# A two-layer FNet and GEGLU kernel on one core: layer 0's last two row blocks multiply by wh as a pair, and accumulators are begun by ScalarE's copies

## The chip, the core and the metric

The program runs on one core of a Trainium2 chip. The core has a matrix engine (TensorE, PE in the profile; its weight loads stand apart as PEld), a vector engine (VectorE, DVE), an activation engine (ScalarE, ACT), a general engine (GpSimd, POOL) and a queue engine that mostly issues DMAs (SyncE, SP). Each engine takes its own instructions in order and waits on semaphores for the others. Tiles lie in SBUF, 128 partitions wide; TensorE writes its products to PSUM, which the program uses as eight banks of 128 x 512 float32, and a group of matmuls may add up in one bank.

The metric is the device time of one execution in microseconds, the median over runs. Less is better.

## The reference

Four layers on x of 2048 rows and 512 columns, float32, each with a layer norm ahead and a residual: Fourier mixing, GEGLU, mixing, GEGLU.

```python
def _layernorm(x, axis=-1, eps=1e-5): ...
def _A_ref(x, dft_seq_re, dft_seq_im, dft_hid_re, dft_hid_im):
    a = einsum("bsd,ed->bse", x, dft_hid_re)
    b = einsum("bsd,ed->bse", x, dft_hid_im)
    return einsum("ts,bse->bte", dft_seq_re, a) - einsum("ts,bse->bte", dft_seq_im, b)
def _B_ref(x, w_gate, w_up, w_down):            # 512 -> 1792 -> 512
    return (_gelu(x @ w_gate) * (x @ w_up)) @ w_down
x = x + _A_ref(_layernorm(x), ...)
x = x + _B_ref(_layernorm(x), ...)
x = x + _A_ref(_layernorm(x), ...)
x = x + _B_ref(_layernorm(x), ...)
```

## The kernel before

**Products.** Every float32 product is made of three matmuls: each operand is split into a high part (a copy by ScalarE to the matmul's type, line 126) and the rest (a subtraction on VectorE, line 128), and `mm3` multiplies high by high, high by low and low by high (lines 166 to 168). A matmul has 128 x 128 weights and mostly 512 moving columns.

**Seven instead of eight.** Most large products are done by Winograd's form of a 2 x 2 block product: seven block products, named A11, A12, S1, S2, S3, S4 and A22, with sums and differences of blocks (`plus`, `minus`, lines 157 and 154, on VectorE) before and after. S1, S2, S3 and S4 are sums of the left operand's blocks, T1 to T4 those of the right one's.

**Mixing (`mix`, layers 0 and 2).** The rows of the result are done in four blocks b = 0 to 3 of 512. First the sequence product, by seven products over NK = 8 chunks: A11 and A12 for all four blocks ahead (in layer 0 in one sweep over the rows, `fore`, 384 matmuls), whose sums for blocks 1 to 3 are put away in DRAM (`put_away`, tensors m and m_sum) and fetched back later; then, block by block, `s2` (S2, S1, S3; 144 matmuls) and `s4` (S4, A22; 96). Where TensorE's product has to be added to an earlier sum, VectorE adds it (`based`, line 157). Then the hidden product by wh: `hid_groups` does a block's four row tiles by eight 128-row chunks of wh, 4 x 8 x 3 = 96 matmuls, into four banks, and `x_add` adds the rows of x and writes them out. Where a block and the next are named in `PAIRED`, the two blocks' products by wh are instead one more 2 x 2 block product (`pair_products`): seven products over four chunks of 128 and two halves, 7 x 4 x 2 x 3 = 168 matmuls. Its right operand's parts lie ready in DRAM (tensor wp), made earlier by `weight_steps`, and its results are transposed by VectorE in 32 x 32 pieces and added to turned rows of x (`turned_rows`). Before, layer 2 has two pairs and layer 0 none.

**Sums of the sequence weights.** A block's S1 to S4 are the same in layers 0 and 2. For the block named in `STORED` layer 0 writes them to DRAM (tensors S1 to S4, 32 writes of 256 KB by GpSimd's queue) and layer 2 loads them; for the others layer 2 forms them anew.

**GEGLU (`geglu`, layers 1 and 3, two halves w = 0 and 1 of 1024 rows).** Gate/up goes over 14 weight blocks n, each seven products of six matmuls: A11 into bank `chain`, S2 on top of it, S1 into `side`, then S3, S4, A12 (`second`) and A22. A11's and A12's product of the next block are done between (`first(n + 1)`, `second(n + 1)`). The split weights of a block are made once, in layer 1's first half (`weight_steps`, four `divide` steps), and written to DRAM (tensor wb) for the three later halves, which load them two blocks ahead (`piece_load`). Down goes the same way, its weights in tensor wc.

**Order.** The program is written as one sequence with side work hung in: after each product `step()` takes one entry from `queue`, and each `PACE`-th time one from `slow`. A planner then lays down each engine's order from modelled durations when the program is built; no engine reorders afterwards (TensorE's weight loads apart). Loads of weights run `AHEAD` and `RAW` items ahead of their use.

## Time and profile before

| | |
|---|---|
| time, median of 3 runs (lowest, highest) | 1589.49 us (1589.01, 1591.12) |
| span of the profiled execution, first to last instruction | 1587.3 us |
| its own time beside the span | not given apart; the median of the runs is 2.2 us above the span |
| TensorE, VectorE, ScalarE, GpSimd busy | 1579.0, 1250.1, 875.4, 253.6 us |
| matmuls in the records | 7000 (22 of them warm the engine up) |
| DMA | 427 MB, 269 GB/s over the span |

By TensorE's count the stages lie in the span about so: layer 0's opening sweep to 95 us, the rest of its mixing to 400 us, layer 1's halves to 600 and 800 us, layer 2's mixing to 1181 us, layer 3's halves to 1381 us and the end. A row of a stretch reads: busy time of each engine with its instructions, then granted clock, DMA share and GB/s. A row of waits names the engine and line that waited, who ended it, total us, times and the longest.

### The profile page before, as it was taken

How to read it: one execution, taken by the hardware profiler on the slowest of the kernel's cores; microseconds unless marked ns; L12 is line 12 of the kernel's file. 1: busy time of each engine (PE TensorE's matmuls, PEld its weight loads, DVE VectorE, ACT ScalarE, POOL GpSimd, SP SyncE). 2: the span in 40 equal slices, each digit the busy share in tenths (PEclk: the TensorE clock that was granted, in tenths of full speed). 3: DMA queues.
4: the chain of work that ended last, by engine and by line, in shares of the span. 5: the costliest groups of instructions: out<-in, count | busy, mean ns of one | idle time of the engine just before them, and what ended most of it. 6: DMA issues, size and time to landing. Idle time of an engine off the chain costs nothing.

```text
span 1587.3 us, 23208 instructions
## 1 busy us (share of the span) xinstructions
PE 1579.0 (99%) x7000; PEld 1307.6 (82%) x7000; DVE 1250.1 (79%) x2174; ACT 875.4 (55%) x1714; POOL 253.6 (16%) x445
## 2 busy tenths in 40 slices
PE   9999999999999999999999999999999999999998
PEld 7888888888888888888888888888888888888887
DVE  8999999889699795566969997869985458754475
ACT  7864574645676652746768444566546435433361
POOL 2200324311465201230031000021002000000001
PEclk9999999999999999999999999999999999999999
DMA  9946989987999999996976785789998967896463
GB/s 360 332 150 232 361 270 362 335 286 259 328 344 345 297 329 301 288 331 221 310 238 217 270 229 172 233 283 309 279 327 239 297 198 238 293 289 197 135 197 81
DMA packets 257660, 427.04 MB, mean 269 GB/s; under 512 B 33344, under 2 KB 89408, under 8 KB 256512
## 3 DMA queue, kind: packets, MB, share of 16 engines
q1 hardware_dynamic: 228560, 333.28, 66.2%
q0 software_dynamic: 26544, 91.51, 15.7%
q8 instruction: 55, 0.90, 0.2%
q10 hardware_dynamic: 2432, 0.79, 0.2%
q14 instruction: 69, 0.57, 0.1%
HBM read 335.02 MB, written 90.44 MB: 268 GB/s over the span
## 4 chain that ended last, share of the span: by engine, by line
PE 96%; DVE 2%; DMA 2%; issue 0%; ACT 0%; SPq 0%; DVEq 0%; ACTq 0%
PE p L166 32%; PE p L167 32%; PE p L168 32%; DMA s<-ws 1%; DVE s L128 1%; DVE s L154 0%; DMA s<-x 0%; DVE s L157 0%; DVE xwide L154 0%; ACT s L126 0%; DVE wide L154 0%; SPq L302 0%; SPq L194 0%; ACT s L572 0%; DVE wide L157 0%
## 5 line engine op out<-in xcount | busy, mean ns | idle before, releaser
L167 PE MATMUL p<-s,s 128*128 128x512 f32 x2326 | 899.8, 388 | 0.0
L168 PE MATMUL p<-s,s 128*128 128x512 f32 x2326 | 887.6, 388 | 0.0
L166 PE MATMUL p<-s,s 128*128 128x512 f32 x2326 | 872.5, 388 | 2.0 <-ACT s L126 1.5
L126 ACT ACTIVATE s<-s 128x512 fp32r<-128x512 f32 (+1 forms) x868 | 487.4, 608 | 319.8 <-DVE s L154 108.7
L128 DVE TENSOR_TENSOR s<-s,s 128x512 fp32r<-128x512 f32 (+1 forms) x868 | 546.0, 669 | 58.2 <-ACT s L126 54.0
L166 PEld LDWEIGHTS p<-s,s 128*128 128x128 f32 x2326 | 436.7, 188 | 94.2 <-ACT s L126 3.4
L167 PEld LDWEIGHTS p<-s,s 128*128 128x128 f32 x2326 | 436.8, 188 | 89.7 <-DVE s L128 0.5
L168 PEld LDWEIGHTS p<-s,s 128*128 128x128 f32 x2326 | 436.6, 188 | 89.4
L157 DVE TENSOR_TENSOR s<-s,p 128x512 f32<-128x512 f32 (+1 forms) x293 | 196.2, 682 | 189.6 <-PE p L168 109.5
L154 DVE TENSOR_TENSOR s<-s,s 128x512 f32<-128x512 f32 (+1 forms) x414 | 249.8, 623 | 2.8 <-DMA s<-ws 0.9
L161 ACT ACTIVATE s<-p 128x512 f32<-128x512 f32 x252 | 146.9, 592 | 147.0 <-PE p L168 142.0
L1079 ACT ACTIVATE s<-s 128x512 f32<-128x512 f32 x112 | 70.3, 629 | 121.5 <-DVE s L157 121.0
L247 POOL DMA_DIRECT2D x<-wide x16 | 10.4, 660 | 374.7 <-DVE wide L157 374.7
L285 POOL DMA_DIRECT2D wb<-s x84 | 45.9, 548 | 100.2 <-ACT s L126 73.3
L1093 DVE TENSOR_TENSOR s<-s,s 128x512 f32<-128x512 f32 x84 | 57.9, 689 | 1.9
L126 ACT ACTIVATE s<-xwide 128x512 fp32r<-128x512 f32 (+1 forms) x52 | 31.0, 613 | 27.5 <-DVE xwide L157 10.0
L572 ACT ACTIVATE s<-s,shift,rstd 128x512 f32<-128x512 f32 x55 | 44.0, 807 | 3.9 <-DVE shift L536 3.2
L157 DVE TENSOR_TENSOR s<-s,s 128x512 f32<-128x512 f32 (+1 forms) x68 | 40.1, 591 | 5.0 <-DMA s<-wgu 3.3
L545 POOL TENSOR_SCALAR rstd<-rstd 128x1 f32<-128x1 f32 x48 | 14.2, 296 | 179.9 <-ACT junk L544 179.1
L285 POOL DMA_DIRECT2D wc<-s x42 | 30.1, 718 | 74.8 <-ACT s L126 53.2
L128 DVE TENSOR_TENSOR s<-xwide,s 128x512 fp32r<-128x512 f32 (+1 forms) x52 | 35.0, 682 | 7.1 <-ACT s L126 7.0
L542 ACT ACTIVATE junk<-s 128x512 f32<-128x512 f32 x45 | 28.1, 623 | 18.7 <-DMA s<-x 18.4
(105 smaller groups left out, 526.8 us busy)
## 6 DMA issues: line engine op xcount, KB each, us to landing
s<-ws SPq DMA_DIRECT2D x348, 256.0 KB, 5.1
s<-wb SPq DMA_DIRECT2D x294, 256.0 KB, 5.4
s<-wc SPq DMA_DIRECT2D x196, 256.0 KB, 4.5
wb<-s POOLq DMA_DIRECT2D x98, 256.0 KB, 5.6
s<-wp SPq DMA_DIRECT2D x56, 256.0 KB, 4.0
wc<-s POOLq DMA_DIRECT2D x49, 256.0 KB, 5.7
s<-x SPq DMA_DIRECT2D x45, 256.0 KB, 5.3
xwide<-x SPq DMA_DIRECT2D x43, 256.0 KB, 8.0
```

The costliest lines, as they stand in the source:

```text
L126: nc.scalar.activation(hi, src, AF.Copy)
L128: nc.vector.tensor_tensor(lo, src, f32(hi), op=ALU.subtract)
L154: nc.vector.tensor_tensor(out, a, b, op=ALU.subtract)
L157: nc.vector.tensor_tensor(out, a, b, op=ALU.add)
L161: nc.scalar.activation(v, src, AF.Copy)
L166: nc.tensor.matmul(ps, ah, bh, start=start, stop=False, skip_group_check=True)
L167: nc.tensor.matmul(ps, ah, bl, start=False, stop=False, skip_group_check=True)
L168: nc.tensor.matmul(ps, al, bh, start=False, stop=stop, skip_group_check=True)
L285: nc.gpsimd.dma_start(to, t)
L572: nc.scalar.activation(z, x, AF.Identity, bias=shift, scale=rstd)
L1079: nc.scalar.activation(t, g, AF.Gelu_apprx_tanh)
L1093: nc.vector.tensor_tensor(t, t, v, op=ALU.mult)
```

## The change

Layer 0: blocks 2 and 3 go through `pair_products` (`PAIRED = {0: (2,), ...}`), so blocks 0 and 1 keep `hid_groups`, with wh split from its plain form each time (the stored tensor wh is gone). The four wp blocks and three wc blocks are made in layer 0 beside blocks 0 and 1 (`made_ahead`, every third step) instead of beside layer 1's second half and block 0. The transposes after layer 0's pair are put off, one a step (`deferred`). The block whose sums are stored is block 0 instead of block 2.

Banks begun by copies (`seeded`): a sum that was added by VectorE after a product is copied into the product's bank by ScalarE before it, and the product adds onto it: the put-away sums (`begin`, loaded by `brought` a little earlier), A12's sums, the rows of x in `hid_groups`, S4's bank in blocks 0 and 1, A12's bank in the pairs, and in gate/up A12's bank, which begins with A11's product. What was then added by VectorE is copied out by ScalarE or read from the bank by the next instruction.

Gate/up blocks 3, 5, 7 and 9 (`ANEW`) are not written to DRAM; each of the three later halves loads their plain weights and forms and splits them anew. In layer 2 the norm of rows 8 to 11 takes VectorE's statistics instead of ScalarE's sums.

```diff
-PACE = 9
+PACE = 9, 3
-BEFORE = {0: (0, 1, 2)}
+BEFORE = 3
+ANEW = 3, 5, 7, 9
-KEEP22 = {0: (2, 3), 2: ()}
-PAIRED = {0: (), 2: (0, 2)}
+KEEP22 = {0: (), 2: ()}
+PAIRED = {0: (2,), 2: (0, 2)}
-STORED = 2,
-BACK_AT = 4, 7
-KEEP_AT = 2
+STORED = 0,
+BACK_AT = 7
+ROWS_AT = 3
...
+    def seeded(src):
+        ps = ps8.get()
+        nc.scalar.activation(ps, src, AF.Copy)
+        return ps
...
-    PAIR_ORDER = [(name, k) for name in ("A11", "A12", "S1", "S2", "S4", "S3", "A22") for k in range(ND)]
+    PAIR_ORDER = [(name, k) for name in ("A11", "S1", "A12", "S2", "S4", "S3", "A22") for k in range(ND)]
...
-        if slow and steps_done[0] % PACE == 0:
+        if deferred:
+            deferred.pop(0)()
+        elif slow and steps_done[0] % pace[0] == 0:
             slow.pop(0)()
...
     def hid_groups(b, groups):
-                hid[b] = [ps8.get() for _ in range(NT)]
+                hid[b] = seeds.pop(b)
...
+                if groups is MID_HID and n == len(groups) - 1:
+                    brought(b + 1)
+                if last and n:
+                    begin(b + 1)
...
-                    x_add(layer, b * NT + i, xrows[i], ps)
+                    t = copied(ps)
+                    ps8.put(ps)
+                    nc.gpsimd.dma_start(rows(layer + 1, b * NT + i), t)
+                    sb.put(t)
...
+        def brought(b):
+            if 0 < b < FORE[layer]:
+                sums[b] = [fetched((layer, b, c)) for c in range(2)]
+        def begin(b):
+            if b < FORE[layer]:
+                chains[b] = [seeded(v) for v in sums[b]]
+                sb.put(*sums.pop(b))
...
     def s2(b):
+                if layer == 0:
+                    pace[0] = PACE[1]
+                    slow.extend(made_ahead())
-            if fore:
-                chains[b] = [ps8.get() for _ in range(2)]
...
-                    us[b] = [based(b, c, p) for c, p in enumerate(chain)]
+                    us[b] = [copied(p, True) for p in chain]
...
+                        if plain_hid(b):
+                            nc.scalar.activation(one[c], v, AF.Copy)
...
     def ended(name, ps):                       # in pair_products
-                if name in ("A11", "S2", "S1"):
+                if name == "A11":
+                    banks["two"] = [seeded(p) for p in ps]
+                elif name in ("S2", "S1"):
                     ys[name] = [copied(p) for p in ps]
...
         def divide(i):
-                if i < 3:
-                    t = split_slot(src[i])
+                t = split_slot(src[i]) if i < 3 else (split_side(v["S4"]),)
+                if place is wblocks and n in ANEW:
+                    pass
+                elif i < 3:
                     kept(to, t, place is not wblocks)
...
+    def made_ahead():
+        steps = []
+        for k in range(ND):
+            steps.append(weight_steps(k, whc, whd))
+            if k < BEFORE:
+                steps.append(down_weight_steps(k))
+        ...
     def geglu(w, layer):
+        else:
+            making.update((n, weight_steps(n)) for n in ANEW)
...
         def first(n):
-                c11[n] = copied(chain[n])
+                c11[n] = seeded(chain[n])
         def second(n):
-                ps = ps8.get()
-                product(n, ps, "A12", "B21", True, True)
-                v = c11.pop(n)
-                plus(v, v, ps)
+                ps = c11.pop(n)
+                product(n, ps, "A12", "B21", False, True)
+                finished(n, 0, 0, ps)
                 ps8.put(ps)
-                finished(n, 0, 0, v)
-                sb.put(v)
...
-            if layer == w == 1 and 0 <= n - WHD_AT < ND and PAIRED[2]:
-                load, runs = weight_steps(n - WHD_AT, whc, whd)
-                load()
-                queue.extend(runs)
```

In the built order of the changed program line numbers move: the three matmul lines are 172 to 174, `seeded` is 167, and the gate/up multiplication is 1137 (1093 before); lines 126, 128, 154, 157 and 161 (`copied`) stay. Names such as s63_7292 or p0_7325 are a slot of SBUF (s) or a bank (p) with the number of its use.

In layer 0 the pair begins so on TensorE, where block 2's and 3's row tiles by wh stood; p1 and p2 are A11's two banks, and the second name in each row is wh's part, of chunk 0 and then 1:

```order
L172 MATMUL p1_4482<-s42_4461,s61_4347 128x512
L173 MATMUL p1_4482<-s59_4462,s61_4347 128x512
L174 MATMUL p1_4482<-s42_4461,s61_4347 128x512
L172 MATMUL p2_4483<-s42_4461,s61_4347 128x512
L173 MATMUL p2_4483<-s59_4462,s61_4347 128x512
L174 MATMUL p2_4483<-s42_4461,s61_4347 128x512
L172 MATMUL p1_4482<-s55_4465,s85_4359 128x512
```

Two banks, c = 0 and 1, each take three matmuls a chunk, and the order goes on with chunk 1.

On ScalarE, at block 1 of layer 1's second half, before and then in the change:

```order
L161 ACTIVATE s74_7138<-p5_7131 128x512
L161 ACTIVATE s57_7147<-p1_7140 128x512
L161 ACTIVATE s71_7129<-p0_7100 128x512
L1079 ACTIVATE s1_7174<-s74_7138 128x512
L1079 ACTIVATE s82_7185<-s71_7129 128x512
```

```order
L126 ACTIVATE s50_7237<-s12_6580 128x512
L167 ACTIVATE p0_7325<-p7_7318 128x512
L161 ACTIVATE s74_7307<-p2_7273 128x512
L161 ACTIVATE s19_7316<-p5_7309 128x512
L126 ACTIVATE s84_7410<-s28_7294 128x512
L126 ACTIVATE s44_7438<-s23_7296 128x512
```

The copy of A11's product goes to bank p0 (line 167) instead of slot s57 (line 161).

More of the change, by code (lines that the diff above doesn't have):

```diff
@@ L204, in x_load_mixed @@
         return t
-    def x_add(layer, i, t, ps, keep=False, engine=nc.gpsimd):
-        plus(t, t, ps)
-        ps8.put(ps)
-        engine.dma_start(rows(layer + 1, i), t)
-        if keep:
-            fresh[i] = t
-        else:
-            sb.put(t)
     xturned = {}
@@ L528, in norm_terms @@
                 for back, which in (1, 0), (2, 1):
-                    if len(terms_made) >= back:
+                    if layer == 0 and len(terms_made) >= back:
                         behind.enter_context(tc.issue_after(terms_made[-back][which]))
@@ L776, in six @@
             step()
-        def based(b, c, ps):
-            if b >= FORE[layer]:
-                return copied(ps, True)
-            v = sb.get(own=True)
-            plus(v, sums[b][c], ps)
-            return v
         def a11(b):
@@ L797, in a12 @@
             stream["more"] = 0
-            side = [ps8.get() for _ in range(2)]
+            if b == NB - 1:
+                begin(0)
+            side = [seeded(v) for v in sums[b]]
             for k in range(NK):
-                six(side, "B21", k, k == 0, k == NK - 1, "21" if b == NB - 1 else None)
+                six(side, "B21", k, False, k == NK - 1, "21" if b == NB - 1 else None)
             for c in range(2):
@@ L811, in a12 @@
                 else:
-                    plus(v, v, side[c])
-                    cs[0, c] = v
+                    sb.put(v)
+                    cs[0, c] = copied(side[c], True)
             ps8.put(*side)
@@ L851, in s2 @@
             for i, k in skewed(3):
-                if b and fore and i == 0 and k == (0 if layer else BACK_AT[0]):
-                    sums[b] = [fetched((layer, b, c)) for c in range(2)]
-                if b and fore and i == 0 and k == (0 if layer else BACK_AT[1]):
+                if plain_hid(b) and i == 0 and k == ROWS_AT:
+                    xrows[b] = [x_load(layer, b * NT + n) for n in range(NT)]
+                if b and fore and i == 0 and k == (0 if layer else BACK_AT):
                     cs.update({(0, c): fetched((layer, b, c, "sum"), True) for c in range(2)})
                 if i == 0:
-                    six(chain, "T2", k, fore and k == 0, k == NK - 1)
+                    six(chain, "T2", k, False, k == NK - 1)
                 elif i == 1:
@@ L890, in s4 @@
                     continue
+                if i == 0 and b in PAIRED[layer]:
+                    begin(b + 1)
                 for c in range(2):
                     if i == 0:
-                        v = cs[0, 2 + c] = sb.get(own=True)
-                        plus(v, u[c], one[c])
+                        if plain_hid(b):
+                            cs[0, 2 + c] = copied(one[c], True)
+                        else:
+                            v = cs[0, 2 + c] = sb.get(own=True)
+                            plus(v, u[c], one[c])
                     else:
@@ L975, in pair_products @@
                     hi, lo = (t[:, h][:, c * P:(c + 1) * P] for h in half)
-                    mm3(banks[bank][c], (hi, lo), parts, name in ("A11", "A12", "S1") and k == 0, k == ND - 1)
+                    mm3(banks[bank][c], (hi, lo), parts, name in ("A11", "S1") and k == 0, k == ND - 1)
                 sb.put(t, *parts)
@@ L1047, in down_weight_steps @@
         return weight_steps(k, wdc, wdd)
-    def down_chores(*ks):
-        steps = [down_weight_steps(k) for k in ks]
-        return [load for load, _ in steps] + [run for _, runs in steps for run in runs]
+    def made_ahead():
[4 more added lines that the diff above has]
+                steps.append(down_weight_steps(k))
+        runs = [steps[0][0]]
+        for (_, todo), after in zip(steps, (*steps[1:], None)):
+            runs += [*todo[:2], *([after[0]] if after else []), *todo[2:]]
+        return runs
     down_making = {}
```

84 lines of the change are left out of this document (49 added, 35 removed).

## The prediction, made before the result was known

> **What bounds the kernel now.** I read the page's first two parts, then TensorE's waits, then the stretches by stage.
>
> ```profile
> span 1587.3 us, 23208 instructions
> PE 1579.0 (99%) x7000; PEld 1307.6 (82%) x7000; DVE 1250.1 (79%) x2174; ACT 875.4 (55%) x1714; POOL 253.6 (16%) x445
> DVE  8999999889699795566969997869985458754475
> PEclk9999999999999999999999999999999999999999
> PE 96%; DVE 2%; DMA 2%; issue 0%; ACT 0%; SPq 0%; DVEq 0%; ACTq 0%
> ```
>
> TensorE is busy for 99% of the span, its granted clock never dips in any slice, and the chain that ended last lies on it for 96%. A busy TensorE may still hide slow matmuls, so I look at its waits and at how many matmuls a stage gets through. The next fence has TensorE's waits, and then stretches of the span: length, busy time of TensorE, its weight loads, VectorE, ScalarE and GpSimd with their instruction counts, granted clock, DMA share, GB/s.
>
> ```profile
> PE p L166 <- ACT s L126: 1.5, 3, 0.8
> PE p L1368 <- POOL ident masks.py:199: 1.4, 1, 1.4
> PE p L166 <- ACT s L1411: 0.5, 1, 0.5
> 95.00:400.00 305.00, 305.00 (x1346) 252.17 (x1345) 278.05 (x475) 166.08 (x318) 72.82 (x130) 1.00 0.83 290
> 600.00:800.00 200.00, 200.00 (x884) 165.61 (x883) 134.16 (x225) 115.76 (x234) 34.46 (x56) 1.00 0.88 283
> 1181.00:1381.00 200.00, 200.00 (x883) 165.50 (x882) 128.53 (x203) 102.12 (x206) 13.21 (x26) 1.00 0.81 251
> 1381.00:1587.00 206.00, 201.37 (x928) 168.34 (x926) 112.90 (x179) 72.40 (x127) 10.34 (x16) 0.99 0.65 188
> ```
>
> The waits, all with ScalarE or GpSimd at their end, come to 3.4 us, nearly all in the opening, which the change leaves as it is. In the rest of layer 0's mixing (95 to 400 us) 1346 matmuls take 305 us, 0.2266 us each; the half layer from 600 to 800 us, other work altogether, has 884 in 200 us, 0.2262 us. So a matmul of 512 columns costs the same wherever it stands, and this kernel's time is a count of matmuls plus the little that TensorE waits. What can spoil it is VectorE, which in places has no time left:
>
> ```profile
> 40.00:200.00 160.00, 160.00 (x707) 132.31 (x706) 153.89 (x297) 98.39 (x182) 28.71 (x43) 1.00 0.76 270
> 840.00:960.00 120.00, 119.65 (x528) 98.77 (x528) 119.61 (x211) 66.63 (x122) 6.36 (x12) 1.00 0.77 245
> 920.00:960.00 40.00, 39.66 (x175) 32.87 (x176) 39.61 (x66) 17.58 (x31) 0.00 (x0) 1.00 0.81 231
> ```
>
> From 40 to 200 us VectorE works 96% of the time and TensorE loses nothing that this view shows. From 840 to 960 us, where layer 2's block 0 forms its sums of weights, VectorE works 119.61 of 120 us, and TensorE loses 0.34 us. That is what a full VectorE costs here: little, as long as it keeps its lead.
>
> **The pair, the main term.** Blocks 2 and 3 of layer 0 had 8 products each by wh, 4 row tiles wide, three matmuls each: 2 x 96 = 192. As a pair they are seven products over four chunks, two halves and three matmuls: 168. The whole program has 6894 matmuls of 512 columns before and 6870 after; no other count on TensorE changes. 24 x 0.2266 us = **5.44 us** off TensorE.
>
> A rule speaks against that price: the Trainium skill's "TensorE: Matmul & The Clock Gate", under Back-to-back issue gap, gives about 131 ns per matmul for a sustained stream at N=512. By it the 24 would be worth 3.1 us, and the time would come to the edge of no change. The two stage rows above have 0.226 us per matmul in a stream without a gap, so the trace disagrees and the sum goes by the trace.
>
> **VectorE, block 0's stored sums and the chores.** Durations come from these groups (busy us, mean ns of one):
>
> ```profile
> L157 DVE TENSOR_TENSOR s<-s,p 128x512 f32<-128x512 f32 x289 | 194.7, 686 | 184.6 <-PE p L168 104.4 <-ACT s L161 77.4 <-DMA s<-wc 1.3
> L128 DVE TENSOR_TENSOR s<-s,s 128x512 fp32r<-128x512 f32 x800 | 521.7, 690 | 53.2 <-ACT s L126 49.1 <-DMA wp<-s 2.2 <-DMA s<-wc 0.7
> L154 DVE TENSOR_TENSOR s<-s,s 128x256 f32<-128x256 f32 x104 | 41.9, 422 | 0.1
> L161 ACT ACTIVATE s<-p 128x512 f32<-128x512 f32 x252 | 146.9, 592 | 147.0 <-PE p L168 142.0 <-DVE s L128 2.3 <-PE p L167 1.5
> L126 ACT ACTIVATE s<-s 128x512 fp32r<-128x512 f32 x800 | 466.7, 625 | 319.1 <-DVE s L154 108.2 <-DVE s L1093 57.2 <-DVE s L157 38.7
> ```
>
> Layer 0 after its opening gains the pair's differences, the four wp blocks and the transposes, and loses additions to ScalarE's copies. Counted in the order that the build makes, its VectorE instructions go from 435 to 448 of 512 elements and from 38 to 49 of 256: 13 x 0.69 + 11 x 0.42 = 13.6 us on 278.05 busy, 291.7 in a stage that is now 299.6 us long, 97.4%. Layer 2 gains where it stood full: with block 0's sums stored, 840 to 960 us sheds its subtractions, and I take the 0.34 us there as gone. But block 2, whose sums used to be stored, now forms them. From 1000 to 1160 us VectorE goes from 234 to 261 instructions, 27 x 0.69 = 18.6 us more, on these four stretches:
>
> ```profile
> 1000.00:1040.00 40.00, 40.00 (x178) 33.13 (x177) 35.40 (x59) 23.01 (x42) 2.61 (x4) 1.00 0.86 287
> 1040.00:1080.00 40.00, 40.00 (x178) 33.16 (x177) 28.34 (x47) 27.97 (x67) 9.83 (x17) 1.00 0.86 266
> 1080.00:1120.00 40.00, 40.00 (x178) 33.12 (x178) 36.74 (x62) 22.28 (x44) 2.37 (x5) 1.00 0.99 296
> 1120.00:1160.00 40.00, 40.00 (x178) 33.00 (x177) 40.00 (x68) 22.82 (x41) 0.00 (x0) 1.00 1.03 311
> ```
>
> 140.5 busy becomes 159.1 of 160 us. So the full stretch moves from block 0 to block 2. At the price of the 840 row, 0.34 us per 120 us, it costs 0.45 us; layer 0, between the 96% row (nothing) and the 100% row (0.85 us), I put at 0.3. Together **0.75 us**, with 0 below and the slow rival above.
>
> **Banks begun by copies.** In gate/up, the addition of A12's product is gone. VectorE in layer 1's second half, block 1, before and then now:
>
> ```order
> L157 TENSOR_TENSOR s71_7129<-s71_7129,p5_7131 128x512
> L157 TENSOR_TENSOR s57_7147<-s57_7147,p2_7187 128x512
> L1093 TENSOR_TENSOR s13_7121<-s13_7121,s57_7147 128x512
> L128 TENSOR_TENSOR s36_7223<-s13_7121,s92_7222 128x512
> ```
>
> ```order
> L157 TENSOR_TENSOR s74_7307<-s74_7307,p5_7309 128x512
> L1137 TENSOR_TENSOR s63_7292<-s63_7292,p0_7325 128x512
> L157 TENSOR_TENSOR s12_7482<-s76_7483,s12_7482 128x256
> L154 TENSOR_TENSOR s54_7481<-s71_7480,s76_7483 128x256
> L154 TENSOR_TENSOR s54_7481<-s12_7482,s71_7480 128x256
> L128 TENSOR_TENSOR s18_7399<-s63_7292,s5_7398 128x512
> ```
>
> The second addition (s57) is gone and the multiplication (L1093, now L1137) reads the bank itself; the 256-wide rows are a block being split anew. TensorE now waits for a copy between A11 and A12. A copy into a bank stands nowhere in this trace; from the nearest rows it takes 0.59 to 0.63 us. Counted in the order, 41 of the 62 copies from one bank to another (gate/up and pairs) have 18 matmuls, 4.1 us, between the bank that they read and the one that they begin, and only one has fewer than ten; the copy with a matmul's end (0.39 us) hides in 4.1 us, on an engine that is 55% busy. The tightest place is block 0 of the same half, TensorE now:
>
> ```order
> L172 MATMUL p2_7273<-s61_6784,s40_6929 128x512
> L173 MATMUL p2_7273<-s42_6785,s40_6929 128x512
> L174 MATMUL p2_7273<-s61_6784,s58_6930 128x512
> L172 MATMUL p0_6666<-s83_6917,s50_6842 128x512
> L172 MATMUL p3_6667<-s83_6917,s50_6842 128x512
> L172 MATMUL p6_5131<-s87_6898,s55_6826 128x512
> L172 MATMUL p1_5132<-s87_6898,s55_6826 128x512
> L172 MATMUL p4_7280<-s69_6800,s40_6929 128x512
> ```
>
> p2 is A11's bank and p4 the one that a copy of it begins. Only four matmuls stand between: p4 may start five steps after the last of p2 did, 1.13 us, against 0.39 + 0.59 to 0.63 and two handoffs. I take 0.2 us lost (0 to 0.4), and if a split were ahead in ScalarE's queue 0.63 more. VectorE has cover: per half layer it loses 14 additions (9.6 us).
>
> The other banks begun by copies wait for loads of layer 0's and 2's put-away sums. The shortest way, block 1 of layer 0, has 36 matmuls from the load's place to the bank's first use: 8.2 us.
>
> ```profile
> s<-m SPq DMA_DIRECT2D x12, 256.0 KB, 5.4
> xwide<-x SPq DMA_DIRECT2D x43, 256.0 KB, 8.0
> ```
>
> At the first row's landing plus 0.6 us the way is free; at the second row's, 0.4 us late, with ScalarE's splits queued behind it. I take 0.
>
> **Four blocks split anew.** Each costs VectorE 4 x 0.42 + 3 x 0.69 + 0.42 = 4.2 us and ScalarE 3 x 0.63 + 0.41 = 2.3 us; four per half, 16.8 and 9.2 us, against the 9.6 us above and, in layer 1's second half, wp's blocks that moved away. VectorE stands idle for 66, 71 and 93 us in those three halves (600, 1181 and 1381 rows): nothing. SP issues 84 fewer loads of wb for 36 of wgu, and GpSimd fewer writes (44 fewer DMAs in all). Block 0's 32 stored writes now fall near 90 to 150 us instead of 240 to 320, when DMAs have room, and the old place shows that they are borne even without it:
>
> ```profile
> 240.00:320.00 80.00, 80.00 (x354) 66.24 (x354) 68.80 (x117) 43.54 (x86) 31.54 (x60) 1.00 0.97 349
> ```
>
> **The sum.** -5.44 - 0.34 + 0.75 + 0.2 = -4.83 us, on the profiled execution's span 1587.3: 1582.5. The median of the runs shown, 1589.49, stands 2.2 us above that span, in what no view shows, and I leave that as it is: 1589.49 - 4.83 = **1584.7 us**.
>
> **The rivals.**
> - *Late loads for begun banks.* All six block changes lose the 0.4 us: 2.4 us, 1587.1, no change that can be told. For it: ScalarE serves in order, so one late load holds its splits too. Against it: medians near 5 us.
> - *VectorE becomes the bound* (slower). Place: 95 to 400 and 1000 to 1160 us. Before, it idled 26.95 and 19.5 us there; some of that is waiting for TensorE and ScalarE that it can't fill, as the idle columns of L157 and L128 show. If half can't be filled, the stages need 291.7 + 13.5 - 299.6 = 5.6 us and 159.1 + 9.8 - 160 = 8.9 us more than TensorE: 14.5 us, 1589.49 - 5.78 + 14.5 + 0.2 = 1598.4. It decides from a loss of 9 us, some two fifths; at a third the losses are 1.1 and 5.6 us, and it is 1590.6, no change. Against it: the 40 to 200 row, with 4% idle, and the 840 row, with none, so hardly any of it is beyond filling. The Trainium skill's "TensorE: Matmul & The Clock Gate" (Part 1: The HAM clock gate) adds that an idle window of about 3.4 us halves the clock; no gap here is that long, and nothing hangs on it.
> - *More than the count.* All that VectorE and the tight bank may lose stays hidden: 1589.49 - 5.78 = 1583.7. It is inside the forecast.
>
> **Chances.** This kernel's runs spread by 0.13%, so about 0.2% (3.2 us) is what can be told from no change. Forecast with less than 2.6 us lost: 0.73. Late loads: 0.07. VectorE at about a third: 0.11; at half: 0.09. So faster 0.73, same 0.18, slower 0.09. The range goes from 1582.8 (nothing lost, a run 0.9 us below its median) up to 1588.8, where it holds the late loads and the milder part of VectorE's case.
>
> **What would show it.** Right: 6976 matmuls on TensorE's row, 1346 in 305 us still, waits of TensorE under 4 us, VectorE near 97% in layer 0 and near 99% from 1000 to 1160 us. Wrong: TensorE waiting for DVE L128 or L157 in those stretches by several us, or for ACT copies (the bank lines), or a step above 0.227 us.

## The result: slower by 12 us, and the profile after

| | before | changed |
|---|---|---|
| time, median (lowest, highest) | 1589.25 us (1588.58, 1591.12) | 1601.44 us (1600.28, 1604.92) |
| ratio, 95% interval | | 1.0076 (1.0062 to 1.009) |
| span of the profiled execution | 1587.3 us | 1598.5 us |
| matmuls | 7000 | 6976 |

The page of the changed kernel, its span, busy times, and the rows of the 40 slices that answer to those shown of before:

```profile
span 1598.5 us, 23040 instructions
PE 1580.6 (99%) x6976; PEld 1305.2 (82%) x6976; DVE 1258.9 (79%) x2222; ACT 929.6 (58%) x1824; POOL 234.9 (15%) x397
DVE  8998989999888796545869587898996547864475
PEclk9999999999999999999999999999999999999999
PE 74%; DVE 2%; DMA 1%; issue 1%; ACT 1%; POOL 0%; SPq 0%; DVEq 0%; ACTq 0%; POOLq 0%
```

TensorE reads 99% busy as before, although it has 24 matmuls fewer: the page's first part hides the loss. The chain shows it, 74% on TensorE where there was 96%. TensorE's waits name ScalarE's split (line 126) and VectorE (lines 157 and 128):

```profile
PE p L172 <- ACT s L126: 8.5, 5, 4.4
PE p L172 <- DVE s L157: 1.4, 1, 1.4
PE p L172 <- DVE s L128: 0.9, 1, 0.9
```

By stretches (length, then busy time of TensorE, its weight loads, VectorE, ScalarE, GpSimd, then clock, DMA share, GB/s) the loss has its places:

```profile
95.00:400.00 305.00, 301.74 (x1322) 248.54 (x1322) 288.48 (x498) 192.11 (x375) 73.34 (x118) 0.99 0.91 310
320.00:360.00 40.00, 37.75 (x160) 30.39 (x159) 39.00 (x66) 29.39 (x61) 8.40 (x14) 0.96 0.87 284
600.00:800.00 200.00, 200.00 (x884) 165.61 (x883) 126.62 (x212) 114.95 (x234) 13.14 (x26) 1.00 0.71 217
840.00:960.00 120.00, 120.00 (x531) 99.38 (x530) 98.72 (x177) 73.79 (x138) 6.17 (x12) 1.00 0.77 247
1000.00:1160.00 160.00, 153.83 (x662) 125.42 (x661) 147.37 (x243) 92.28 (x186) 17.59 (x26) 0.98 0.89 279
1040.00:1080.00 40.00, 35.57 (x143) 28.43 (x143) 38.28 (x64) 24.59 (x54) 9.97 (x13) 0.92 0.78 244
```

From 1040 to 1080 us TensorE got through 143 matmuls where it had 178, and the granted clock fell to 0.92: beside the 4.4 us in which it stood still, eleven matmuls behind the stall took 0.427 us each instead of 0.227; from 320 to 360 us it is the same on a smaller scale. Halves of layers 1 and 3 (600 to 800 us) are as before, 884 matmuls in 200 us.

I make the account of every run in one way: of each step from one matmul's start to the next that is longer than 0.30 us, what exceeds 0.2267 us, added up by stage. This includes the slow matmuls behind a stall. The four columns are layer 0 after its opening (95 to 400 us), layer 1 (400 to 800), layer 2 to 980 us (block 0), and layer 2 from 980 to 1180 us.

| lost, us | layer 0 | layer 1 | layer 2, to 980 | layer 2, from 980 | median, us |
|---|---|---|---|---|---|
| before | 0.1 | 0 | 0.6 | 0 | 1589.25 |
| changed | 5.4 | 1.9 | 0 | 10.2 | 1601.44 |

So 17.5 us against 0.7: 16.8 us more, less 5.44 us for the matmuls and 0.6 us in the opening, is 10.8 of the 11.2 us between the two spans. The profiled execution of the changed kernel (1600.28 us) is the fastest of its four; what the others lost beyond it was not seen.

### The profile page after: what moved, and what is told of

Same layout as the page of the kernel before. It is cut to its first block, busy times and chain, and to the rows that moved or that the text cites. A ratio compares the mean times of both kernels' runs of the same rounds, so it can differ in the third digit from the quotient of the medians.

```text
span 1598.5 us, 23040 instructions
## 1 busy us (share of the span) xinstructions
PE 1580.6 (99%) x6976; PEld 1305.2 (82%) x6976; DVE 1258.9 (79%) x2222; ACT 929.6 (58%) x1824; POOL 234.9 (15%) x397
## 4 chain that ended last, share of the span: by engine, by line
PE 74%; DVE 2%; DMA 1%; issue 1%; ACT 1%; POOL 0%; SPq 0%; DVEq 0%; ACTq 0%; POOLq 0%
PE p L173 25%; PE p L174 25%; PE p L172 25%; DVE s L128 1%; DVE s L154 1%; DMA s<-wc 1%; DMA s<-wb 0%; DVE s L157 0%; ACT s L126 0%; POOL rstd L533 0%; DMA s<-ws 0%; ACT junk L532 0%; DVE s L236 0%; SPq L209 0%; ACT s L560 0%
## 5 line engine op out<-in xcount | busy, mean ns | idle before, releaser
L173 PE MATMUL p<-s,s 128*128 128x512 f32 (+1 forms) x2318 | 898.6, 389 | 0.4 <-DVE s L128 0.3
L174 PE MATMUL p<-s,s 128*128 128x512 f32 (+1 forms) x2318 | 887.5, 388 | 0.0
L172 PE MATMUL p<-s,s 128*128 128x512 f32 (+1 forms) x2318 | 866.4, 389 | 11.3 <-ACT s L126 8.5
L126 ACT ACTIVATE s<-s 128x512 fp32r<-128x512 f32 (+1 forms) x930 | 521.2, 607 | 291.4 <-DVE s L154 97.1
L128 DVE TENSOR_TENSOR s<-s,s 128x512 fp32r<-128x512 f32 (+1 forms) x930 | 582.0, 662 | 109.8 <-ACT s L126 103.5
L154 DVE TENSOR_TENSOR s<-s,s 128x512 f32<-128x512 f32 (+1 forms) x486 | 286.2, 608 | 4.2 <-DMA s<-wgu 0.9
L157 DVE TENSOR_TENSOR s<-s,p 128x512 f32<-128x512 f32 (+1 forms) x212 | 141.4, 677 | 132.8 <-PE p L174 131.6
L1123 ACT ACTIVATE s<-s 128x512 f32<-128x512 f32 x84 | 52.9, 630 | 58.5 <-DVE s L157 57.8
L1137 DVE TENSOR_TENSOR s<-s,p 128x512 f32<-128x512 f32 x56 | 38.3, 683 | 33.6 <-PE p L174 33.4
L167 ACT ACTIVATE p<-p 128x512 f32<-128x512 f32 x62 | 36.1, 583 | 47.9 <-PE p L174 31.8
L157 DVE TENSOR_TENSOR s<-s,s 128x512 f32<-128x512 f32 (+1 forms) x86 | 49.1, 572 | 4.9 <-DMA s<-wdc 1.9
L149 ACT ACTIVATE s<-s 128x512 fp32r<-128x512 f32 x50 | 30.6, 627 | 23.1 <-DVE s L154 10.0
L533 POOL TENSOR_SCALAR rstd<-rstd 128x1 f32<-128x1 f32 x44 | 16.8, 383 | 171.1 <-ACT junk L532 170.5
L1137 DVE TENSOR_TENSOR s<-s,s 128x512 f32<-128x512 f32 x56 | 38.5, 689 | 1.3
```

The lines of the kernel that those rows point to most:

```text
L126: nc.scalar.activation(hi, src, AF.Copy)
L128: nc.vector.tensor_tensor(lo, src, f32(hi), op=ALU.subtract)
L154: nc.vector.tensor_tensor(out, a, b, op=ALU.subtract)
L157: nc.vector.tensor_tensor(out, a, b, op=ALU.add)
L167: nc.scalar.activation(ps, src, AF.Copy)
L172: nc.tensor.matmul(ps, ah, bh, start=start, stop=False, skip_group_check=True)
```

## The experiments

Kernels that ran together share their runs of the kernel before; ratios are to those. Each was planned anew when it was built, so a stall can also shift with the edit.

### First set: one part undone, or one part alone

e1, both blocks' sums stored:

```diff
-STORED = 0,
+STORED = 0, 2
```

> The changed kernel with block 2's sums stored as well as block 0's (layer 0 writes 32 more tiles, layer 2 loads them). VectorE loses about 27 subtractions between 1000 and 1160 us. Theory 1 (VectorE has too much to do in layer 2's block 2): the excess steps of TensorE at 1031, 1069 and 1131 us, together 9.7 us with the half clock behind them, go: 1601.4 - 9.7 = 1591.7 us, and those in layer 0 (5.9 us) and at 560 to 575 us (2.75 us) stay. Theory 2 (late loads and banks begun by copies make the stalls): the added loads help nothing there, 1601 us or more. Theory 3 (GpSimd's one-column instruction held by VectorE makes the one long stall at 1069 us): that stall shrinks only where VectorE's run has a pause; without one, 1599 to 1601 us.

Measured 1599.79 us, ratio 1.0054 (1.0039 to 1.007). Layer 2 lost 4.2 us instead of 10.2, but layer 0 lost 10.8 instead of 5.4. In this kernel's stretch from 240 to 280 us the DMA engines are full:

```profile
240.00:280.00 40.00, 40.00 (x178) 33.03 (x176) 35.71 (x62) 23.19 (x43) 22.72 (x39) 1.00 1.01 384
```

Theory 1 holds for layer 2, and something the theories had not named costs as much in layer 0.

e2, the pair undone:

```diff
-PAIRED = {0: (2,), 2: (0, 2)}
+PAIRED = {0: (), 2: (0, 2)}
```

> The changed kernel without the pair in layer 0: blocks 2 and 3 multiply by wh in row tiles again, 24 matmuls more, 5.4 us, all else as in the change. Theory 1 (VectorE is too full in layer 0, the pair's differences among its work): the stalls at 280 and 336 us (5.9 us) go, 1601.4 + 5.4 - 5.9 = 1600.9 us, and layer 2's stalls stay. Theory 2 (begun banks and late loads make layer 0's stalls): they stay without the pair, 1606.8 us.

Measured 1604.09 us, ratio 1.0083 (1.0068 to 1.0099). Layers 0 and 1 lost nothing at all (5.4 and 1.9 before the edit): the pair's own stalls cost 7.3 us and eat its gain of 5.44. Layer 2, whose source is the same though its order was laid down anew, lost 16.1 us instead of 10.2, so what layer 2 loses is not a fixed sum: in the kernels with that source (this one, e12, e14, e16 and e18) it lies between 8.6 and 16.1 us. A difference of a few us in layer 2 therefore shows nothing by itself.

e3b, the norm's scale on VectorE:

```diff
-            nc.gpsimd.tensor_scalar(rstd, rstd, 1.0 / D, EPS, op0=ALU.mult, op1=ALU.add)
+            nc.vector.tensor_scalar(rstd, rstd, 1.0 / D, EPS, op0=ALU.mult, op1=ALU.add)
```

> The changed kernel with the first of the norm's one-column instructions (line 533, scale and add epsilon) on VectorE instead of GpSimd. Theory 3 (held by VectorE's run for 2.5 us at 1066 us, with ScalarE waiting behind it): TensorE's stall of 4.4 us at 1069 us falls to about 2 us and the half clock behind it (2 us) goes: 1597 us. Theory 1 alone (VectorE is late there anyway): the same wait shows up on VectorE's own instruction, 1600 to 1602 us.

This theory came from the chain of the changed kernel ahead of its longest stall (start, us, what):

```profile
1060.29 2.36 DMA s<-ws
...
1064.98 0.71 ACT junk L532 x2
...
1065.85 2.68 POOL rstd L533
...
1068.60 0.57 POOL rstd L534
...
1069.43 0.58 ACT s L126
```

Line 533 takes 0.19 us as a rule and took 2.68 us there, with ScalarE's splits queued behind what waits for it. Measured: 1600.66 us, ratio 1.0048 (1.0029 to 1.0067). The stall stayed as long, a step of 4.59 us, and TensorE now waited for VectorE:

```profile
PE p L172 <- DVE s L157: 7.2, 3, 4.2
```

GpSimd's slow instruction was on the chain, but VectorE was as late without it. As the only cause the theory falls. Two things stay open: the single times lie at 1596.6 and 1597.1 us and at 1600.7 to 1601.9, and the profile is one of the latter, while 1597 us is what the theory had forecast; and in e2, e12, e14, e16 and e18 an instruction held for 2.66 to 2.67 us stands again ahead of a step of 4.72 to 4.77 us.

e4, the kernel before, with block 0's sums stored instead of block 2's and nothing else:

```diff
-STORED = 2,
+STORED = 0,
```

> The kernel before with one part of the change alone: block 0's sums are stored in layer 0 instead of block 2's, so layer 2 forms block 2's sums between 1000 and 1160 us and sheds block 0's. Theory 1: layer 2's losses of the change appear here by themselves, 9.7 - 0.4 us: 1598.5 us, with excess steps of TensorE between 1020 and 1135 us and VectorE at 98 to 100% there. Theory 2 (banks begun by copies): no such bank is in this kernel, so 1589 us.

Measured 1599.71 us, ratio 1.0053 (1.0035 to 1.0071), all of it in layer 2 (11.9 us lost from 980 us on, nothing elsewhere):

```profile
1040.00:1080.00 40.00, 36.52 (x147) 29.28 (x147) 38.10 (x64) 26.01 (x60) 11.01 (x15) 0.91 0.78 235
1120.00:1160.00 40.00, 37.47 (x159) 30.57 (x158) 38.49 (x65) 19.09 (x35) 0.00 (x0) 0.96 1.00 290
```

One line of the change, with no bank begun by a copy, costs 0.53% where the whole change costs 0.76%. Where block 2's sums are formed in layer 2 is enough to bring that layer's loss (11.9 us here, 10.2 in the change).

### Second set: why was that line changed?

e7, neither the pair nor the new stored block, all else of the change kept (`STORED = 2,` and `PAIRED = {0: (), 2: (0, 2)}`):

> The changed kernel without the pair in layer 0 and with block 2's sums stored as before; the banks begun by copies, the four blocks split anew, and wp and wc made beside blocks 0 and 1 stay. Theory 1 (VectorE too full, by the pair in layer 0 and by block 2's sums in layer 2): with both gone all stalls go, and 24 matmuls are back: the time of the kernel before, within 0.2%. Theory 2 (begun banks and late loads stall TensorE by themselves): stalls of several us stay, 1595 us or more beside a kernel before of 1590.

Measured 1604.88 us, ratio 1.0076 (1.0054 to 1.0098): theory 1 missed by 13 us. Layer 0 lost 15.1 us, most of it in one stall at 302 us and the slow matmuls behind it. The waits, the chain ahead of it, and two stretches:

```profile
PE p L172 <- ACT s L126: 10.3, 4, 9.2
```

```profile
298.95 7.03 DMA s<-ws
...
306.04 4.89 DMA s<-wh
```

```profile
240.00:280.00 40.00, 40.00 (x178) 33.14 (x177) 33.22 (x57) 22.05 (x41) 17.89 (x31) 1.00 1.03 392
280.00:320.00 40.00, 28.67 (x112) 22.33 (x111) 26.98 (x47) 25.03 (x55) 10.60 (x19) 0.83 0.82 303
```

VectorE is not full here. A DMA share of 1.03 comes first, then two loads in a row that are late. The loads of ws that SP issues from 230 to 285 us land after 7.1 us in the median, where those of the changed kernel land after 5.2 (each kernel's DMA issues in that window):

```profile
s<-ws SPq DMA_DIRECT2D x21, 256.0 KB, 7.1
```

```profile
s<-ws SPq DMA_DIRECT2D x36, 256.0 KB, 5.2
```

The kernel before writes these sums at the same place, and was at the limit there:

```profile
240.00:280.00 40.00, 40.00 (x178) 33.10 (x178) 36.32 (x61) 18.43 (x32) 16.69 (x31) 1.00 1.00 363
```

In layer 0 the change now makes wp and wc beside blocks 0 and 1, with their reads and writes, and block 2's 32 writes fall on top of these.

e8, block 2's sums stored instead of block 0's, the pair kept (`STORED = 2,`):

> The changed kernel with block 2's sums stored instead of block 0's, as in the kernel before; the pair stays. Theory 1: the stalls from 1020 to 1135 us go (9.7 us of excess steps), VectorE is full at 840 to 960 us again at the price of 0.4 us, and layer 0 keeps its 5.9 us: 1592 us. Theory 4 (in layer 0 the DMA engines, not VectorE, are what is full: block 2's 32 writes fall at 240 to 320 us, where the run that stored both blocks' sums had a DMA share of 1.04 and lost 11 us): layer 0 loses 10 us or more, 1597 us.

Measured 1599.05 us, ratio 1.0055 (1.0032 to 1.0078). Layer 2 lost 3.2 us instead of 10.2, layer 0 in the profiled execution 6.6. The single times of this kernel lie at 1593.5 to 1595.6 and at 1602.5 to 1603.0 us, with nothing between; the profile fell on the fastest. What the others lost was not seen.

e9, every second chunk of block 2 stored too:

```diff
-STORED = 0,
+STORED = {(0, k) for k in range(8)} | {(2, k) for k in range(1, 8, 2)}
```

> The changed kernel with the sums of every second chunk of block 2 stored as well as all of block 0's: 16 more writes in layer 0, and 12 or 13 subtractions fewer in layer 2's block 2, 9 us of VectorE. Theory 1: the stalls from 1020 to 1135 us fall from 9.7 to under 3 us. Theory 4: layer 0's losses lie between those of the change (5.9 us) and those with both blocks stored (11 us). Together 1593 to 1598 us.

Measured 1596.8 us, ratio 1.0039 (1.0021 to 1.0056). Layer 2 still lost 6.5 us, twice what was expected, layer 0 only 2.0, layer 1 7.5: stalls were traded for others. (The profiled execution took 1599.97 us, 3.2 above the median.)

The first probe:

> Not the layers: the whole computation is left out. First 40 bursts of 60 matmuls (128 x 512), with pauses between them made by chains of copies on ScalarE, from about 1.7 to 4.5 us. The clock theory: after pauses up to about 2 us a burst starts at 0.227 us a step, after longer ones (2.6 us and more) with about 10 steps of 0.427 us; the border shows the idle time that it takes. Rival: the slow steps follow the place in the program or VectorE's load, not the pause, and no burst has them, or all have. Then runs of 0 to 8 VectorE instructions of 128 x 512 with one one-column GpSimd instruction free to start with the first of them. The hold theory: it ends with the end of the VectorE run (2 instructions 1.4 us, 8 instructions about 4.9 us) where both operands lie in SBUF, and takes 0.2 us where one lies in PSUM or where VectorE transposes. Rival: it takes 0.2 us in all of them.

39 pauses could be read. By the pause from the last matmul's start to the next one's: 1.74 and 2.08 us, no slow steps in any of 9; 2.42 us, in 3 of 5; 2.76 and 3.10, in 2 of 5 each; 3.44, in 3 of 5; 3.78 and 4.47, in all 10. There are 7 to 14 slow steps, most of 0.427 us, so 1.4 to 2.8 us more. In 7 of these 20 bursts one to six matmuls took 0.23 us before the first of 0.427. Two bursts after the same pause of 2.42 us, and one after 3.78 us:

```profile
191.10:198.50 7.40, 5.37 (x24) 4.12 (x23) 0.00 (x0) 1.84 (x4) 0.00 (x0) 1.00 0.00 0
298.90:306.30 7.40, 5.37 (x17) 3.95 (x16) 0.00 (x0) 1.85 (x4) 0.00 (x0) 0.77 0.00 0
576.40:583.80 7.40, 4.50 (x11) 3.54 (x12) 0.00 (x0) 2.62 (x8) 0.00 (x0) 0.65 0.00 0
```

24 matmuls at clock 1.00 and 17 at 0.77, behind pauses of the same length. The clock theory stands: a stall costs up to 2.8 us more than its length, and between 2.4 and 3.5 us the same pause may bring this or not. In the second part the GpSimd instruction took 0.62 us beside two operands in SBUF, however long the run, and 0.19 us beside one in PSUM or a transpose: the hold theory is half right.

### Third set: is it the load of layer 0?

e12, the sums of wp and wc replaced by copies on ScalarE in layer 0:

```diff
         def sums():
+            if raw is whc or raw is wdc and n < BEFORE:
+                for name, of in (("S1", "A22"), ("S2", "A11"), ("S3", "A21"), ("S4", "A12")):
+                    nc.scalar.activation(v[name], v[of], AF.Copy)
+                return
```

> The changed kernel, with the 28 sums and differences of 256 columns that make the parts of wp and of the first three wc blocks in layer 0 replaced by copies on ScalarE: the same loads, splits and writes, 11.8 us less on VectorE before 280 us, and wrong weights in layers 0, 1 and 3 (the sums are what it leaves out). Theory 1 (VectorE full in layer 0): the stalls at 280 and 336 us (5.9 us with the half clock) fall below 2 us, and layer 2 keeps its 9.7: 1597 us. Theory 4 (the DMA engines, or loads that wait for slots held by writes): the same DMAs, the same stalls, 1601 us.

Measured 1600.34 us, ratio 1.0065 (1.0048 to 1.0081). The stall at 280 us was gone; that at 335 us stayed (4.0 us). Relief of VectorE up to 280 us did not carry over to 335.

e13 and e14, two wc blocks made in layer 1 (`BEFORE = 1`, block 1 begun ahead of gate/up block 0, two queue entries a step where more than seven wait), with block 2's and with block 0's sums stored:

> A version meant to be faster: the pair stays, block 2's sums are stored (layer 2 as before), and two of the three wc blocks are made in layer 1's first half instead of layer 0, which takes 8.4 us off VectorE and some 3.8 MB of DMA out of 95 to 280 us. If the pair's stalls come from what layer 0 has to carry (VectorE and DMA together), it loses at most 4 us there, 1 to 3 us in layer 2: 1587 to 1590 us, beside 1589 to 1592 of the kernel before. If the 32 writes of block 2's sums fill the DMA engines at 240 to 280 us by themselves (share over 1.0 again), layer 0 loses 8 us or more: 1595 to 1600 us.

> The same move of two wc blocks, with block 0's sums stored as in the change. Layer 0: VectorE and DMA both eased, so its 5.9 us fall below 2; layer 2 as in the change, 9.7 us lost: 1597 us. If it is 1601, what layer 0 loses is not a matter of its load.

Measured 1598.94 us, ratio 1.0059 (1.0044 to 1.0074), and 1611.85 us, ratio 1.0145 (1.0129 to 1.0162). The stall at 335 us stayed in both (layer 0 lost 2.3 and 4.8 us), with layer 0 eased ahead of it in the second, and layer 1, to which the work had moved, lost 7.0 and 12.5 us; layer 2 lost 7.5 and 14.8. From the second run, the stretches ahead of the stall and around it:

```profile
240.00:320.00 80.00, 80.00 (x355) 66.26 (x354) 69.28 (x117) 39.35 (x76) 4.61 (x9) 1.00 0.72 229
300.00:340.00 40.00, 37.37 (x161) 30.31 (x160) 36.10 (x64) 28.59 (x63) 9.38 (x17) 0.98 0.83 284
```

Neither VectorE (69.28 of 80) nor the DMA engines (0.72) are full in the 80 us ahead, and TensorE stalls all the same.

The second probe:

> Not the layers: the whole computation is left out. Runs of 4, 8 and 12 VectorE instructions of 128 x 512 (both operands in SBUF with a float32 result; the same with the matmul's type as result; one operand in PSUM; the two results in turn) and one one-column GpSimd instruction that becomes free 0.8 to 2.6 us into the run. In the first probe it ended with the first VectorE instruction (0.62 us); in the kernels it was held through runs of 4 to 6. Hold theory: started in the middle of a run it lasts to the end of the run, so longer the earlier it starts and the longer the run (up to 6 us with 12), with both operands in SBUF, and 0.2 us with one in PSUM. Rival: it waits for one VectorE instruction at most, 0.7 us, in all runs, and what held it in the kernels is something else.

GpSimd's instruction ended 0.05 us after the end of the VectorE instruction that ran when it started, in runs of 4, 8 and 12 alike (0.38 to 0.63 us while a run was on); with an operand in PSUM it took 0.19 us. Three starts into runs of 12:

```profile
58.72 0.50 POOL L52 TENSOR_SCALAR r<-late 128x1 f32<-128x1 f32 x1 [9.16 <-ACT late L50]
68.34 0.44 POOL L52 TENSOR_SCALAR r<-late 128x1 f32<-128x1 f32 x1 [9.13 <-ACT late L50]
77.97 0.38 POOL L52 TENSOR_SCALAR r<-late 128x1 f32<-128x1 f32 x1 [9.19 <-ACT late L50]
```

The rival holds: one instruction, not the run. What kept GpSimd for 2.68 us in the kernel is open.

### Fourth set: VectorE's instructions alone, the writes alone, the side work alone

e15, layer 2's block 2 without its sums:

```diff
-            plus(s1, a21, a22)
-            minus(a21, a11, a21)
-            minus(a11, s1, a11)
+            if (layer, b) != (2, 2):
+                plus(s1, a21, a22)
+                minus(a21, a11, a21)
+                minus(a11, s1, a11)
...
-            minus(a12, a12, v)
+            if (layer, b) != (2, 2):
+                minus(a12, a12, v)
```

> The changed kernel without the 32 sums and differences that make block 2's S1 to S4 in layer 2 (they are left out, the loads, splits and products stay, so layer 2's result is wrong): 22 us of VectorE less between 1000 and 1160 us, the same DMAs. Theory 1 (VectorE): excess steps from 1020 to 1135 us fall from 9.7 to under 1.5 us, the rest stays: 1592 us. Theory 4 (loads late there): they stay, 1600 us.

Measured 1600.4 us, ratio 1.0074 (1.0052 to 1.0095). The stalls at 1031 and 1069 us went (the step of 4.77 us is one of 1.40), but a stall of 5.1 us came at 1124, and layer 2 lost 9.5 us. VectorE's waits from 1030 to 1095 us, and its stretch after that:

```profile
DVE s L128 <- ACT s L126: 14.1, 2, 12.9
DVE wide L653 <- ACT s L562: 3.1, 2, 2.1
DVE wide L653 <- DMA t<-wide: 3.1, 1, 3.1
```

```profile
1090.00:1130.00 40.00, 34.14 (x150) 27.62 (x149) 40.00 (x67) 21.14 (x37) 1.50 (x2) 1.00 0.96 283
```

With 32 instructions fewer, VectorE stood idle for 12.9 us in one piece, behind ScalarE, and then worked 40.00 of 40 us with TensorE waiting. ScalarE itself waited 10.7 us there for a product of TensorE's that it was to copy next (line 161): both engines had run as far ahead as their fixed orders let them. Time that VectorE was given in block 2 could not be used for block 3's sums. In its strict form theory 1 falls: without the sums the stall at 1069 us is gone, but taking them away is not enough. How full VectorE is does not tell the cases apart: from 1000 to 1160 us it is busy for 128.97 us here and 129.39 in e8, where the sums come ready from DRAM, and layer 2 lost 9.5 and 3.2 us; and from 1090 to 1130 us the kernel before has it busy for 39.09 of 40 and loses nothing.

e16, layer 0's block 3 without half its sums (the same edit on S3 and S4 for layer 0, block 3):

> The changed kernel without 16 of the 32 sums of block 3 in layer 0 (S3's and S4's, left out, the rest stays): 11 us of VectorE less between some 285 and 340 us, the same DMAs. Theory 1 in its narrow form (VectorE is full in the 50 us ahead of the stall, since the pair took the products by wh from between block 2 and block 3, and relief further ahead does not carry): the stall at 335 us (4.6 us with the half clock) goes, 1596 to 1597 us, while those at 560 to 575 and in layer 2 stay. Theory 4 (loads, slots): the stall stays.

Measured 1601.21 us, ratio 1.0067 (1.0043 to 1.0091). The stall stayed, with VectorE at 31.17 of 40 us:

```profile
300.00:340.00 40.00, 38.59 (x171) 31.62 (x169) 31.17 (x55) 26.99 (x61) 8.20 (x16) 1.00 0.90 305
```

So VectorE's load by itself does not make the stall in layer 0. The chain ahead of the stall goes through the norm's steps and a load that SP issued late (start, us, what):

```profile
327.27 0.71 ACT s L562
...
328.01 0.72 DVE wide L653
328.73 0.42 SPq L253
...
330.92 5.50 DMA s<-ws
336.41 0.28 DVE s L128
```

e17, half the writes in the kernel with neither pair nor new stored block:

```diff
             for name, t in tiles.items():
-                nc.gpsimd.dma_start(stored[b, k, name], t)
+                if name in ("S1", "S2"):
+                    nc.gpsimd.dma_start(stored[b, k, name], t)
```

> The run without the pair and with block 2's sums stored (1604.9 us, a stall of 9.6 us at 302 us behind late loads of ws and wh), with only 16 of its 32 writes: S3's and S4's are left out, and layer 2 loads S1 and S2 in their place, so its result is wrong; nothing else changes. Theory 4 for that kernel (the DMA engines are full at 240 to 280 us, share 1.03, by these writes): the share falls below 1 and the 13 us go: 1591 us. If it is not the writes, the stall stays, 1600 us or more.

Measured 1590.72 us beside 1589.93, ratio 1.0003 (0.9991 to 1.0016), the ten times within 1590.45 and 1592.7. Layer 0 lost nothing:

```profile
240.00:280.00 40.00, 40.00 (x179) 33.11 (x178) 32.90 (x58) 21.61 (x41) 13.92 (x23) 1.00 0.96 347
280.00:320.00 40.00, 40.00 (x178) 33.15 (x177) 34.19 (x61) 31.75 (x71) 10.02 (x18) 1.00 0.90 318
```

16 writes fewer, and some 12 us less beside the kernel before (1.0003 against 1.0076). The writes are the cause of that kernel's stall. The run also has all banks begun by copies, the four blocks split anew, and wp and wc made in layer 0: together these cost 0.5 us, 2.5 at most by the interval, with half the stored writes of the kernel before.

e18, the side work spread that the program takes from `queue` beside block 3 (two loads of weights, the norms of layer 1's rows, and the making of its first weight block):

```diff
-                queue.extend([run for chore in chores_at(b) for run in (chore, None)])
+                queue.extend([run for chore in chores_at(b) for run in (chore, *[None] * 3)])
```

> The changed kernel with layer 1's norms and the two loads queued with them (side work beside block 3's products in layer 0) spread over twice as many steps, so that more of it falls beside the pair's products. Theory 1 in its narrow form: VectorE is eased ahead of 335 us and the stall there shrinks from 4.6 us to 2 or less; 1598 us if nothing is given back at layer 1's start, where these norms are needed. If what is put off is missing at 395 to 400 us, a stall appears there and the time is 1601 us or more.

Measured 1597.35 us, ratio 1.0043 (1.0028 to 1.0058). The stall at 335 us is gone, although VectorE is as full there as in the changed kernel (38.95 of 40 beside 39.00), and nothing appears at layer 1's start:

```profile
320.00:360.00 40.00, 40.00 (x179) 33.10 (x178) 38.95 (x67) 29.42 (x63) 7.60 (x14) 1.00 0.91 294
```

This names that stall: layer 1's side work, which the pair has pushed beside block 3's products since there are no more products by wh of block 2 to put it beside. Which of its parts counts, the norms on the chain of e16 or the rest, was not tried apart. A stall at 280 us (2.5 us) remained.

### Fifth set: can the pair's gain be had?

e19 and e20, the side work spread, and block 2's sums stored for every second chunk or for all, none of block 0's:

> The changed kernel with the norm's side work spread as in the run before, and with the stored sums those of every second chunk of block 2 (none of block 0's): 16 writes in layer 0. If each stall goes with its own cause: layer 0 loses 1 to 3 us (280 us), layer 1 about 1.5, layer 2 about 5: 1592 to 1594 us, still not under the kernel before. If the stalls move on instead of going, 1597 us.

> The same with all of block 2's sums stored, 32 writes. If 32 writes fill the DMA engines at 240 to 280 us by themselves: share over 1.0 there, 8 us or more lost between 280 and 340 us, layer 2 losing about 3: 1597 to 1600 us. If the DMA stall needed the crowded side work too: 1590 to 1592 us.

Measured 1595.66 us, ratio 1.0034 (1.0022 to 1.0046), and 1597.63 us, ratio 1.0047 (1.0031 to 1.0064). With 16 writes layer 0 lost nothing, for the first time with the pair in it; layer 1 lost 4.3 us and layer 2 8.1. With 32 writes the DMA share was 1.02 at 240 to 280 us again and layer 0 lost 7.0 us, layer 2 5.5. Most of the 7.0 us is one stall of 4.4 us at 335 us, behind a load of ws that took 4.3 us, and the slow matmuls after it: in the place that e18 had cleared. So the stall of the 32 writes does not need the crowded side work. Layer 2's loss goes with how many of block 2's sums it forms, and not with how many it forms in all: with none 0.6 to 7.5 us (the kernel before, e1, e7, e8, e13, e17, e20), with half 6.5 and 8.1 (e9, e19), with all 8.6 to 16.1, while e20 forms as many in all as the changed kernel. (e15, which leaves block 2's sums out, lost 9.5.) No version came below the kernel before.

## Why the prediction was wrong, step by step

The time, 1601.44 us, lies 12.6 us above the range.

**The pair, -5.44 us: right.** 6976 matmuls at the same 0.2267 us.

**VectorE at 840 to 960 us, -0.34: right.** 98.72 busy of 120 us, TensorE 120.00.

**VectorE, +0.75 us: the step that failed.** It stood for 0.45 us from 1000 to 1160 us, where 10.2 were lost, and 0.3 in layer 0, where 5.4 were. The failure has two parts. First, the price: "That is what a full VectorE costs here: little, as long as it keeps its lead" was read off 40 to 200 and 840 to 960 us, where VectorE is full of work that has its inputs. In block 2 of layer 2 it shares the chain with a norm on ScalarE and with loads, and it could not even be as busy as forecast: 147.37 us of 160 against the 159.1 counted. Nor did TensorE's waits name VectorE, as the prediction's sign of this case had it: 8.5 us of them ended with ScalarE's splits (line 126), 1.4 and 0.9 with VectorE. Idle time that can't be filled was the slow rival, given a chance of 0.09. Its places and sizes were near: 8.9 us in block 2 and 5.6 in layer 0 at half, and 10.2 (2.2 of it the half clock) and 5.4 measured; that they are so near is in part luck, since kernels with the same source in layer 2 lost 8.6 to 16.1 us, and layer 0's loss turned out to have another mechanism. e4 shows that forming block 2's sums there is enough for layer 2's loss. That VectorE's load alone makes it is not shown: e15 took that load away and lost 9.5 us. What else in forming the sums there stops TensorE, such as the loads and the order laid down, stays open.

Second, the measure. Layer 0 was counted as 291.7 us of 299.6, over the whole stage; it came to 288.48 of 305. The stall at 335 us did not follow that total (e12, e14, e16) but where layer 1's side work lies (e18). The diff shows that with the pair no products by wh are left between block 2 and block 3, and I did not ask what had run beside them.

**"Nothing hangs on it": wrong.** The prediction cited the Trainium skill's "TensorE: Matmul & The Clock Gate" for a clock halved after an idle window of about 3.4 us and said that no gap is that long. Steps of 2.64 and 4.77 us came, and the 7 and 11 matmuls behind them at 0.43 us or a little more cost 3.6 of the 17.5 us.

**Banks begun by copies, +0.2, and late loads, 0: right in size.** The tight place in layer 1's second half lost nothing (600 to 800 us: 200.00 of 200). A copy from bank to bank took 0.58 us. In e17 all of it with the rest costs 0.5 us beside the kernel before (2.5 at most), 2.0 us of stalls in layer 2 among it.

**Four blocks split anew, 0: right.** Layer 1's second half and layer 3's first run at 884 matmuls in 200 us.

**Block 0's stored writes at 90 to 150 us: right, and half the matter.** They cost nothing there, and nothing in e4, where the place of the stored writes is all that is new in layer 0. But the prediction took the old place as proof that writes are borne at 240 to 320 us. They were borne in the kernel before (363 GB/s, share 1.00 at 240 to 280 us); in e7, where wp and wc are made in layer 0 too, they no longer are (392 GB/s, 1.03, 15.1 us lost). The stored block was moved out of a full DMA into a full VectorE, and the kernel loses at either place.

**Layer 1, 1.9 us: not foreseen and not settled.** At 560 to 575 us TensorE waits behind loads of wc and wb; these stalls went with the pair in e2, but e20 has the pair and lost nothing in layer 1. Layer 1 lost more where work was moved into it (7.0 and 12.5 us in e13 and e14), but also where none was (7.5 and 4.9 us in e9 and e12).

## What to carry to other kernels

Price a full engine by a place with the same neighbours, not by any place where it is full: an engine that waits for others between its instructions cannot make up later what it did not do earlier. When work is taken away, ask what had run in its cover, and when work is moved, which resource it had been kept away from; here 32 writes had a choice between a full DMA and a full VectorE. Count a stall that reaches about 2.4 us with up to 2.8 us of slow matmuls on top. And where every edit lays the order down anew, read an edit's effect against kernels with the same source in that stage: here these differ by up to 7.5 us.

## What the runs showed of the hardware

**The clock.** Idle pauses of 2.42 to 3.44 us (start to start) halved TensorE's speed in 10 of 20 cases, pauses up to 2.08 us in none of 9, from 3.78 us in all of 10; 7 to 14 matmuls then took 0.427 us. The Trainium skill's page named above (Part 1: The HAM clock gate) describes a free-running window of 3413 ns and a clock halved after an idle one. The 0.427 us agree with it, and so does that the same pause may or may not do it; a pause of 2.42 us, shorter than the window, that halves the clock does not.

**GpSimd beside VectorE.** A one-column GpSimd instruction, 0.19 us alone, ends 0.05 us after the end of a VectorE instruction with two operands in SBUF, and is not held by one with an operand in PSUM. The Trainium skill's "SBUF — State Buffer" (SBUF: two separate sides) says that the two share a pair of ports under a lock that is held for a whole instruction. The probes agree: 0.63 us at most, less than one VectorE instruction (0.69 us). The 2.68 us of the changed kernel is some four VectorE instructions long, and no run here explains it.

**DMA.** With 16 writes more at 240 to 280 us (e7 beside e17) the share goes from 0.96 to 1.03 and the rate from 347 to 392 GB/s, the median load of ws lands after 7.1 us instead of 5.1, and a stall of 9.6 us comes. The share alone does not decide it: the changed kernel runs at 1.02 and 389 GB/s from 120 to 160 us, and e13 at 1.03 and 382 GB/s from 240 to 280 us, and TensorE loses nothing there.
